# Both row-form attention products of groups 3 to 8 back to back, with three PSUM pairs in rotation

## The chip, the cores and the metric

One core of one Trainium2 chip. The metric is the device time of one execution in microseconds (us), lower is better. "Span" is the time from the first to the last instruction in a trace; it is about 1.8 us less than the timed value of the same execution. All runs told here were in the fast state, at a mean granted clock (the share of its full clock that TensorE was given) of 0.988 or more, and every kernel that ran gave the correct result.

## The reference

An attention without softmax, then a two-layer network with ELU. Batch 8, 8 heads, 576 positions, head size 64; 4608 tokens of 512 features, hidden size 2048.

```python
kv  = np.einsum('bhsd,bhse->bhde', k, v)
out = np.einsum('bhsd,bhde->bhse', q, kv)
rms = np.sqrt(np.mean(out * out, axis=-1, keepdims=True) + 1e-06)
x   = (out / rms * g_norm)              # per head; then tokens x 512
h   = x @ w_in                          # 512 -> 2048
g   = np.where(h > 0, h, np.exp(np.minimum(h, 0)) - 1)
y   = g @ w_out                         # 2048 -> 512
```

## The kernel before

The tokens are worked in nine groups T = 0 to 8 of 512. A "window" of group T holds its first matrix product (eight pairs of feature tiles M0 to M7, `mm1`; a pair is 2 x 128 of the 2048 hidden features, eight matmuls of 512 columns), the second product of group T-1 and half of its own (`mm2_half`, eight matmuls each), and the attention of group T+1: the kv product of batch T+1, and two attention products, halves h = 0 and 1 of the group ("row form": tokens in the PSUM partitions). Each half is squared (ScalarE, ACT), summed (VectorE, DVE), turned into an inverse root (ACT) and scaled (DVE); the scaled rows are transposed by DMA and multiplied by the gain (DVE). A group's tokens can lie in two batches, because a batch has 9 slots of 64 positions and a group 8 slots. Where a pair of slots lies in two batches, its matmul of shape 64x128 (rows x columns of the array in use) is made as two of shape 64x64:

```python
def se_mm(T, h, se_ps):
    for i in range(2):
        (b0, j0), (b1, j1) = (slot_of(T, 4 * h + 2 * i + t) for t in range(2))
        parts = [(0, P, b0, j0, 2)] if b0 == b1 else [(0, 64, b0, j0, 1), (64, P, b1, j1, 1)]
        for m in range(4):
            u, s = m // 2, m % 2
            for l in range(2):
                for lo, hi, b, j, n in parts:
                    nc.tensor.matmul(
                        se_ps[lo:hi, l, (4 * i + m) * 64 : (4 * i + m) * 64 + 64],
                        lhsT=qT[b][l * 64 : l * 64 + 64, s, u, j : j + n, :],
                        rhs=kv_of(b, l, u, s), start=True, stop=True)
```

In PSUM, where matmuls leave their results, the kernel holds tiles of 512 columns: pairs A and B for feature tiles, one pair (here called C, tag "at") for all attention products, two single tiles for the second product's output. The window, shortened:

```python
def window(T, at, early, late, second, relu=(), opened=()):
    for i in range(8):
        ...                                       # (group 2 has its first pair half done)
        rest = mm1(T, i, "BA"[i % 2], i in relu)  # matmuls, then ACT's exp (and relu)
        for name in early.get(i, ()): at[name]()
        if i in second: second[i]()
        rest()                                    # DVE's part of the ELU
        for name in late.get(i, ()): at[name]()

# groups 3 to 7; group 2 has its own lists
early = {2: ("sum0", "inv0"), 4: ("sum1", "inv1"), 5: ("gain0",), 7: ("gain1",)}
late  = {0: ("kv",), 1: ("se0",), 2: ("mul0",), 3: ("se1",), 4: ("mul1", "ahead")}
halves = {0: 1, 1: 3, 2: 4, 3: 5, 4: 6, 5: 7}
# "ahead": DMA transposes of q of batch T+2, then a load of batch T+3
```

## Time and profile before

| | before |
|---|---|
| time, median of the 4 runs beside the changed kernel | 285.95 us (285.7 to 286.31) |
| span of the profiled run | 284.3 us |
| TensorE busy | 97% |
| chain that ended last on TensorE | 84% |

The lines behind the last two are in the prediction. The profile by window follows: length in us, then the busy time of each engine with its instruction count, granted clock, share of the DMA engines, GB/s. The stretches are the windows of groups 2 to 7, from the first matmul of M0 to the next.

```profile
70.72:96.20 25.48, 24.55 (x223) 12.20 (x225) 16.65 (x23) 15.17 (x21) 5.69 (x10) 1.00 0.98 187
96.20:125.53 29.33, 29.03 (x230) 13.52 (x233) 19.78 (x23) 13.57 (x19) 6.64 (x13) 1.00 0.88 175
125.53:154.99 29.46, 29.20 (x236) 13.63 (x240) 18.34 (x22) 13.58 (x19) 5.39 (x11) 1.00 0.72 153
154.99:184.32 29.33, 29.17 (x229) 13.54 (x232) 18.88 (x23) 13.57 (x19) 4.06 (x8) 1.00 0.67 158
184.32:213.78 29.46, 29.20 (x236) 13.63 (x240) 18.59 (x22) 13.58 (x19) 0.00 (x0) 1.00 0.28 66
213.78:242.30 28.52, 28.36 (x157) 12.92 (x160) 18.59 (x22) 13.21 (x18) 0.00 (x0) 1.00 0.28 56
```

The first busy column is TensorE. Groups 3 and 5 take 29.33 us, groups 4 and 6 0.13 us more: their attention has eight matmuls more, for slots in two batches. Group 7 has no kv product. Some matmul records are missing from some traces, which is why counts of equal windows differ by a few; the lengths don't depend on it.

### The profile page before, as it was taken

What the parts mean: (1) busy time and instruction counts of PE and PEld (TensorE: products, weight loads), DVE (VectorE), ACT (ScalarE), POOL (GpSimd) and SP (SyncE); (2) the same over time, 40 slices, a digit from 0 to 9 for tenths busy, and PEclk for the clock granted to TensorE, in tenths of its full rate; (3) what the DMA queues carried; (4) which work ended last, traced back from release to release, by engine and by line L of the source; (5) the groups of instructions that cost most, each with busy time, mean ns of one, the idle gap of its engine ahead of it and who ended that gap; (6) DMA issues with size and microseconds to landing.
All of it is one profiled execution on the core that took longest, in us unless ns stands there. A gap on an engine that the chain in (4) does not pass through costs nothing.

```text
span 284.3 us, 5120 instructions
## 1 busy us (share of the span) xinstructions
PE 274.6 (97%) x2089; PEld 129.1 (45%) x2123; DVE 164.8 (58%) x222; ACT 141.5 (50%) x209; POOL 49.9 (18%) x89
## 2 busy tenths in 40 slices
PE   7899999999899999999999999999999999999994
PEld 3434444444544444444444444444444444444443
DVE  3449532877567657754785378627863786344600
ACT  3778359594568255435542555345543554333311
POOL 7743303341034033032103210000000000000000
PEclk9999999999999999999999999999999999999999
DMA  7999999997999889679637971712150234020222
GB/s 209 193 204 206 205 260 240 202 246 113 184 273 145 165 204 226 83 173 264 149 37 173 256 165 34 157 37 74 39 111 0 74 39 111 0 76 0 74 74 75
DMA packets 50571, 39.46 MB, mean 139 GB/s; under 512 B 30964, under 2 KB 44020, under 8 KB 50548
## 3 DMA queue, kind: packets, MB, share of 16 engines
q0 software_dynamic: 15008, 21.30, 37.4%
q1 hardware_dynamic: 35136, 17.31, 29.5%
q10 hardware_dynamic: 404, 0.53, 0.5%
q8 instruction: 16, 0.26, 0.4%
q14 instruction: 7, 0.06, 0.1%
HBM read 36.70 MB, written 9.44 MB: 162 GB/s over the span
## 4 chain that ended last, share of the span: by engine, by line
PE 84%; DMA 7%; DVE 3%; SPq 2%; issue 1%; ACT 1%; POOL 0%; DVEq 0%; POOLq 0%
PE h_ps L382 39%; PE o_ps L403 39%; DMA w_in_sb<-in_moe_w_in_dram 3%; DMA v_bf<-in_v_dram 2%; DMA qT<-q_bf 2%; PE at L250 2%; PE at L156 1%; PE o_ps L440 1%; PE h_ps L569 1%; DVE xs L299 1%; DVE ss L283 1%; SPq L331 1%; DVE gT L366 1%; DVE elu_e L362 1%; PE qt_ps L174 0%
## 5 line engine op out<-in xcount | busy, mean ns | idle before, releaser
L403 PE MATMUL o_ps<-w_out_sb,gT 128*128 128x512 bf16 x548 | 128.5, 379 | 0.7 <-issue 0.2
L382 PE MATMUL h_ps<-xT,w_in_sb 128*128 128x512 bf16 (+1 forms) x540 | 126.4, 376 | 1.0
L350 ACT ACTIVATE elu_e<-h_ps 128x1024 bf16<-128x1024 f32 (+1 forms) x79 | 74.0, 952 | 89.6 <-PE h_ps L382 78.4
L403 PEld LDWEIGHTS <-gT 128*128 128x128 bf16 x560 | 54.3, 98 | 66.0 <-issue 0.9
L366 DVE TENSOR_TENSOR gT<-elu_e,h_ps 128x1024 bf16<-128x1024 bf16 (+1 forms) x67 | 77.2, 1157 | 6.9 <-PE h_ps L382 0.5
L382 PEld LDWEIGHTS <-w_in_sb 128*128 128x128 bf16 x560 | 53.2, 98 | 61.1 <-issue 0.2
L362 DVE TENSOR_SCALAR elu_e<-elu_e 128x1024 bf16<-128x1024 bf16 x72 | 31.4, 437 | 65.1 <-ACT elu_e L350 65.0
L419 ACT COPY o_sb<-o_ps 128x512 f32<-128x512 f32 x32 | 18.3, 587 | 20.8 <-PE o_ps L403 20.1
L103 POOL CAST q_bf<-st_q 128x384 bf16<-128x384 f32 x36 | 18.5, 557 | 37.6 <-DMA st_q<-in_q_dram 37.6
L283 DVE TENSOR_REDUCE ss<-sq 128x16 f32<-128x1024 bf16 x14 | 17.1, 1218 | 7.7 <-ACT sq L277 7.7
L299 DVE TENSOR_TENSOR xs<-at,ss 128x1024 bf16<-128x1024 f32 x14 | 17.1, 1219 | 1.9 <-ACT ss L292 1.9
L277 ACT ACTIVATE sq<-at 128x1024 bf16<-128x1024 f32 x14 | 14.4, 1029 | 1.1 <-PE at L250 1.1
L212 DVE SCALAR_TENSOR_TENSOR xT<-y_ps,g_col,rT 128x512 bf16<-128x512 f32 (+1 forms) x10 | 6.2, 641 | 10.2 <-ACT rT L209 7.9
L339 POOL COPY gate<-qT 1x16 bf16<-1x16 bf16 x5 | 1.1, 218 | 60.4 <-DMA qT<-q_bf 60.4
L355 ACT ACTIVATE elu_h<-h_ps 128x1024 bf16<-128x1024 f32 (+1 forms) x12 | 9.3, 817 | 0.0
L156 PEld LDWEIGHTS <-k_bf 64*64 64x64 bf16 x576 | 6.4, 107 | 5.4 <-issue 5.4
L90 POOL DMA_DIRECT2D v_bf<-in_v_dram x11 | 7.8, 708 | 4.2 <-DMA w_in_sb<-in_moe_w_in_dram 2.1
L90 POOL DMA_DIRECT2D k_bf<-in_k_dram x11 | 7.9, 718 | 3.1 <-DMA w_in_sb<-in_moe_w_in_dram 2.4
L312 DVE TENSOR_SCALAR xT<-xT,g_col 128x1024 bf16<-128x1024 bf16 x14 | 6.7, 480 | 1.9 <-DMA xT<-xs 1.9
L250 PEld LDWEIGHTS <-qT 64*128 64x128 bf16 (+1 forms) x248 | 4.5, 97 | 7.1 <-issue 5.9
L250 PE MATMUL at<-kv_sb,qT 64*128 64x64 bf16 (+1 forms) x248 | 6.5, 193 | 0.8 <-DMA qT<-q_bf 0.7
L366 DVE TENSOR_TENSOR gT<-elu_e,elu_h 128x1024 bf16<-128x1024 bf16 x9 | 6.5, 723 | 0.8
(57 smaller groups left out, 94.8 us busy)
## 6 DMA issues: line engine op xcount, KB each, us to landing
st_q<-in_q_dram POOLq DMA_DIRECT2D x6, 1152.0 KB, 8.1
out_dram<-o_sb SPq DMA_DIRECT2D x24, 256.0 KB, 3.4
k_bf<-in_k_dram POOLq DMA_DIRECT2D x6, 576.0 KB, 10.6
v_bf<-in_v_dram POOLq DMA_DIRECT2D x6, 576.0 KB, 13.3
out_dram<-o_sb SPq DMA_DIRECT2D x19, 128.0 KB, 2.4
w_out_sb<-in_moe_w_out_dram POOLq DMA_DIRECT2D x4, 512.0 KB, 15.0
w_in_sb<-in_moe_w_in_dram POOLq DMA_DIRECT2D x2, 512.0 KB, 11.2
q_bf<-in_q_dram POOLq DMA_DIRECT2D x3, 288.0 KB, 13.4
```

The lines of the kernel that those rows point to most:

```text
L90: eng.dma_start(out=dst.rearrange("p m j d -> p m (j d)"), in_=in_[:, ms, :])
L103: nc.gpsimd.tensor_copy(out=bf["q", b][:, u, js], in_=raw[b][:, u::2, js, :].rearrange("p l j d -> p j l d"),)
L250: nc.tensor.matmul(se_ps[lo:hi, l, (4 * i + m) * 64 : (4 * i + m) * 64 + 64], lhsT=qT[b][l * 64 : l * 64 + 64, s, u, j : j + n, :], rhs=kv ...
L277: nc.scalar.activation(sq, st["se", h], AF.Square)
L283: nc.vector.reduce_sum(out=ss, in_=st.pop(("sq", h)).rearrange("p l (m e) -> p (l m) e", e=D), axis=AX.X,)
L299: nc.vector.tensor_tensor(out=st["xs"][:, 2 * h : 2 * h + 2, :].rearrange("p i (l m e) -> p l i m e", l=2, e=D), in0=se_ps.rearrange("p l ...
L350: nc.scalar.activation(e[:, lo:hi, :], h, AF.Exp)
L362: nc.vector.tensor_scalar(out=e, in0=e, scalar1=1.0, scalar2=1.0, op0=ALU.min, op1=ALU.subtract)
L366: nc.vector.tensor_tensor(out=gT[T][:, 2 * i + lo : 2 * i + hi, :], in0=e[:, lo:hi, :], in1=h, op=ALU.add if relu else ALU.max,)
L382: nc.tensor.matmul((ps[a] if isinstance(ps, list) else ps[:, a, :])[:, cols], lhsT=w_in_sb[:, c, f * P : f * P + P], rhs=xT[T][:, c, cols] ...
L403: nc.tensor.matmul(o_ps[T, j], lhsT=gT[T][:, f, j * P : j * P + P], rhs=w_out_sb[:, f, :], start=(f == 0), stop=(f == FC - 1),)
L419: nc.scalar.copy(o_sb[T, half][:, j % 2, :], o_ps[T, j])
```

## The change

Intent: make both attention products of a window one block, after three feature pairs (four in group 2), so that TensorE changes between the wide 128-row matmuls and the 64-row attention matmuls once per window instead of twice. The two halves then need two PSUM pairs at once; one is C, the other is A (B in group 2), and in return C takes one feature pair, so that A, B and C rotate. The core of the diff, shortened:

```diff
-        def se(h):
-            def product():
-                st["se", h] = at_tile()
+        def se(h):
+            def product(tag="C"):
+                st["se", h] = pair(tag, "se_ps")
                 se_mm(T, h, st["se", h])
+
+            def square():
                 ...
-    def window(T, at, early, late, second, relu=(), opened=()):
-        ...
+    def window(T, steps):
+        for step in steps.split():
+            # M<i><pair>: first product and exp; R: with relu on ACT; E<i>: DVE's part of the ELU
+            # H<n>/h<n>: eight matmuls of the second product, of group T-1 / T
+            # K<batch><pair>: kv product; G<h>: gain; Q: transposes of q, next loads
+            # X<pair>: both products (half 0 in <pair>, half 1 in C), sq0 sq1 sum0 sum1 inv0 inv1
+            # Y: both scales and their DMA transposes
+        if T == 2:
+            steps = "M0B K3C E0 M1A H5 E1 M2B E2 R3A H6 E3 XB Y H7 Q M4A E4 h0 R5B E5 M6C G0 E6 M7A G1 E7 h2"
+        elif T + 1 < NT:
+            steps = f"M0B {kv} H1 E0 M1A H3 E1 M2B H4 E2 H5 XA Y H6 Q M3B H7 E3 M4A E4 M5C E5 M6B G0 E6 M7A G1 E7 h0 h2"
```

(The comments on the steps are added here; in the source the letters are the branches of an if.) The last group's window keeps its order.

More of the change, by code (lines that the diff above doesn't have):

```diff
@@ L124, in load_w_out @@
         )
-    def at_tile():
-        return ps_at.tile([P, 2, 512], FP32, name="at", tag="at")
     def single(tag, name):
@@ L135, in pair @@
             return [single(t, name) for t in (tag + tag)[:2]]
+        if tag == "C":
+            return ps_at.tile([P, 2, 512], FP32, name=name, tag="at")
         return ps_m1.tile([P, 2, 512], FP32, name=name, tag=tag)
@@ L256, in se_mm, with kv_all @@
                         )
+    def kv_all(b, tag):
+        kv_ps = pair(tag, "kv_ps")
+        for u in range(2):
+            kv_mm(b, [kv_ps[:, s, :] for s in range(2)], u)
+        return lambda: nc.scalar.copy(
+            kv_sb[:, b], kv_ps[:, :, 0:P].rearrange("p s (u e) -> p u s e", u=2)
+        )
     def attention(T):
         st = {}
-        def kv():
-            if T == B:
-                return
-            kv_ps = at_tile()
-            for u in range(2):
-                kv_mm(T, [kv_ps[:, s, :] for s in range(2)], u)
-            nc.scalar.copy(
-                kv_sb[:, T], kv_ps[:, :, 0:P].rearrange("p s (u e) -> p u s e", u=2)
-            )
         def se(h):
-            def product():
-                st["se", h] = at_tile()
+            def product(tag="C"):
+                st["se", h] = pair(tag, "se_ps")
                 se_mm(T, h, st["se", h])
+            def square():
                 sq = attp.tile([P, 2, DM], BF16, name="sq", tag="sq")
@@ L318, in gain @@
                 )
-            return product, sums, inv, scale, gain
-        pieces = {"kv": kv}
+            return product, square, sums, inv, scale, gain
+        pieces = {}
         for h in range(2):
-            for name, piece in zip(("se", "sum", "inv", "mul", "gain"), se(h)):
+            for name, piece in zip(("se", "sq", "sum", "inv", "mul", "gain"), se(h)):
                 pieces[f"{name}{h}"] = piece
@@ L710 @@
         if i == 3:
-            at["kv"]()
+            kv_all(2, "C")()
         if i == 4:
             at["se0"]()
+            at["sq0"]()
             freed[4]()
@@ L725 @@
     at["se1"]()
+    at["sq1"]()
     freed[7], rest[7] = elu(1, 7, ps, "later")
@@ L750 @@
     at["gain1"]()
-    def window(T, at, early, late, second, relu=(), opened=()):
-        for i in range(8):
-            if i < len(opened):
-                mm1_part(T, i, opened[i], range(KC), slice(256, 512))
-                rest = elu(T, i, opened[i], False)
-            else:
-                rest = mm1(T, i, "BA"[i % 2], i in relu)
-            for name in early.get(i, ()):
-                at[name]()
-            if i in second:
-                second[i]()
-            rest()
-            for name in late.get(i, ()):
-                at[name]()
@@ L769 @@
-    for T in range(2, NT):
-        at, early, late = {}, {}, {}
-        if T + 1 < NT:
-            at = attention(T + 1)
-            if T + 2 < B:
-                cast_q(T + 2)
-                def ahead(b=T + 2):
-                    turn_q(b)
-                    if b + 1 < B:
-                        after_turn(b)
-                        fetch_ahead(b + 1)
-                at["ahead"] = ahead
-            else:
-                at["ahead"] = lambda: None
-            early = {2: ("sum0", "inv0"), 4: ("sum1", "inv1"), 5: ("gain0",), 7: ("gain1",)}
-            late = {0: ("kv",), 1: ("se0",), 2: ("mul0",), 3: ("se1",), 4: ("mul1", "ahead")}
-        if T == 2:
-            early = {2: ("sum0", "inv0"), 5: ("sum1", "inv1", "mul1"), 6: ("gain0",), 7: ("gain1",)}
-            late = {0: ("kv",), 1: ("se0",), 2: ("mul0",), 4: ("se1",), 5: ("ahead",)}
-        halves = {1: 5, 3: 6, 5: 7} if T == 2 else {0: 1, 1: 3, 2: 4, 3: 5, 4: 6, 5: 7}
-        second = {i: (lambda n=n: mm2_half(T - 1, n)) for i, n in halves.items()}
-        if T > 2:
-            window(T, at, early, late, second)
-        else:
-            g_tile(T)
-            opened = [pair("B", "h_ps")]
-            mm1_part(T, 0, opened[0], range(KC), slice(0, 256))
-            window(T, at, early, late, second, (3, 5), opened)
-        mm2_half(T, 0)
-        mm2_half(T, 2)
@@ new lines, in mm1_rest @@
+    def mm1_rest(T, i, tag, relu):
+        mm1_part(T, i, opened, range(KC), slice(256, 512))
+        return elu(T, i, opened, relu)
+    def window(T, steps):
+        rest = {}
+        nxt = attention(T + 1) if T + 1 < NT else None
+        for step in steps.split():
+            kind, arg = step[0], step[1:]
+            if kind in "MR":
+                i, tag = int(arg[0]), arg[1]
+                make = mm1_rest if T == 2 and i == 0 else mm1
+                rest[i] = make(T, i, tag, kind == "R")
+            elif kind == "E":
+                rest.pop(int(arg))()
+            elif kind == "H":
+                mm2_half(T - 1, int(arg))
+            elif kind == "h":
+                mm2_half(T, int(arg))
+            elif kind == "K":
+                kv_all(int(arg[0]), arg[1])()
+            elif kind == "X":
+                nxt["se0"](arg)
+                nxt["se1"]("C")
+                for name in ("sq0", "sq1", "sum0", "sum1", "inv0", "inv1"):
+                    nxt[name]()
+            elif step == "Y":
+                nxt["mul0"]()
+                nxt["mul1"]()
+            elif step == "Q":
+                b = T + 2
+                if b < B:
+                    turn_q(b)
+                if b + 1 < B:
+                    after_turn(b)
+                    fetch_ahead(b + 1)
+            elif kind == "G":
+                nxt[f"gain{arg}"]()
+            else:
+                raise ValueError(step)
@@ new lines @@
+    g_tile(2)
+    opened = pair("B", "h_ps")
+    mm1_part(2, 0, opened, range(KC), slice(0, 256))
+    for T in range(2, NT):
+        if T + 2 < B:
+            cast_q(T + 2)
+        if T == 2:
+            steps = "M0B K3C E0 M1A H5 E1 M2B E2 R3A H6 E3 XB Y H7 Q M4A E4 h0 R5B E5 M6C G0 E6 M7A G1 E7 h2"
+        elif T + 1 < NT:
+            kv = f"K{T + 1}C" if T + 1 < B else ""
+            steps = (
+                f"M0B {kv} H1 E0 M1A H3 E1 M2B H4 E2 H5 XA Y H6 Q M3B H7 E3 M4A E4 M5C E5 M6B G0 E6 M7A G1 E7 h0 h2"
+            )
+        else:
+            steps = "M0B H1 E0 M1A H3 E1 M2B H4 E2 M3A H5 E3 M4B H6 E4 M5A H7 E5 M6B E6 M7A E7 h0 h2"
+        window(T, steps)
```

## The prediction

> **What bounds the kernel now.** I read the page first: busy shares, the slices, the chain that ended last.
>
> ```profile
> PE 274.6 (97%) x2089; PEld 129.1 (45%) x2123; DVE 164.8 (58%) x222; ACT 141.5 (50%) x209; POOL 49.9 (18%) x89
> PEclk9999999999999999999999999999999999999999
> PE 84%; DMA 7%; DVE 3%; SPq 2%; issue 1%; ACT 1%; POOL 0%; DVEq 0%; POOLq 0%
> ```
>
> TensorE (PE) is busy in 97% of the 284.3 us span, at a granted clock that never falls, and carries 84% of the final chain. DVE and ACT have 40 to 50% of their time free. So a change can only gain what TensorE does not spend on streaming columns. Next I read the waits of TensorE. After the start-up, one is left:
>
> ```profile
> PE at L250 <- DMA qT<-q_bf: 0.7, 1, 0.7
> ```
>
> Then the TensorE timeline, one group's window at a time. A window of group T holds eight pairs of feature tiles (call them M0 to M7, 8 matmuls each, L382), the second matrix product of group T-1 and the start of T's own (pieces of 8, L403), the kv product of batch T+1 (L156) and the two attention products of group T+1 (L250, halves h=0 and h=1).
>
> ```profile
> 75.01 1.89 PE L403 MATMUL o_ps<-w_out_sb,gT 128*128 128x512 bf16 x8
> 76.83 0.75 PE L250 MATMUL at<-kv_sb,qT 64*128 64x64 bf16 x13
> 78.26 0.28 PE L250 MATMUL at<-kv_sb,qT 64*64 64x64 bf16 x11 [0.68 <-DMA qT<-q_bf]
> 78.47 3.63 PE L382 MATMUL h_ps<-xT,w_in_sb 128*128 128x512 bf16 x15
> ...
> 102.19 1.89 PE L403 MATMUL o_ps<-w_out_sb,gT 128*128 128x512 bf16 x8
> 104.01 0.41 PE L250 MATMUL at<-kv_sb,qT 64*128 64x64 bf16 x16
> 104.35 1.90 PE L382 MATMUL h_ps<-xT,w_in_sb 128*128 128x512 bf16 x8
> 106.09 1.89 PE L403 MATMUL o_ps<-w_out_sb,gT 128*128 128x512 bf16 x8
> ```
>
> Columns: start, length, what. Eight matmuls take 106.09 - 104.35 = 1.74 us where an attention block stands ahead, 1.727 elsewhere (start to start 0.216 us each in the trace). At full load 102.19 + 1.727 = 103.92 would be the next start; the block starts at 104.01. So entering the block leaves 0.096 us (last matmul to first of the block 0.312 instead of 0.216). Leaving it, the last small matmul is followed after 0.123 us, where inside the block small matmuls follow each other every 0.0145 us: another 0.108. The windows are otherwise full: for group 3 it lasts 125.53 - 96.20 = 29.33 us, of which 128 x 0.2158 = 27.62 are wide matmuls.
>
> The first part, at 76.83, is the one real hole: the block takes 78.47 - 76.83 = 1.64 us where the same block of 24 matmuls elsewhere takes 0.48 (140.69 to 141.17). It waits 1.16 us for the transposed q of batch 3, which lands about 78.2.
>
> **What the Trainium skill says.** "TensorE: Matmul & The Clock Gate", section "Wait — 56ns, not 53.3ns?", gives 215.7 ns between 512-column matmuls at full clock; the trace has 0.216, so there is nothing to gain inside the runs. "TensorEngine Tiling (Array Packing)", "Key Properties": changing the tiling mode drains the TensorE. The attention matmuls use 64 rows, the wide ones 128; the 0.096 and 0.108 us at the edges agree. They also match one exposed weight load (98 ns in the load rows), and I cannot tell the two apart here. "Perfetto Trace Analysis" advises rotating independent matmul groups through different PSUM banks so that the evacuation of one overlaps the next. The kernel before does so with two pairs, A and B, for feature tiles, and keeps a third (C) for attention alone; the change lends C to the feature tiles.
>
> **The change part by part.** The built programs have equal counts on every engine: 72 kv matmuls, 32 or 40 attention matmuls, 128 wide ones in a full window. Only order and PSUM pairs change, in the windows of groups 2 to 7 (products of groups 3 to 8); before 76.8 us and in the last group's window TensorE's order is the same. In the windows of groups 3 to 7 the kv block moves ahead of eight matmuls of the second product: same two edges, no cost.
>
> *Removed, in six windows:* one entry and one exit of an attention block, 0.096 + 0.108 = 0.20 us. Check by sum: two blocks of 16 add 2 x (0.312 + 0.217 + 0.123 - 0.216) = 0.87 us to the stream; one of 32 adds 0.312 + 0.450 + 0.123 - 0.216 = 0.67. All on the path, as TensorE has no slack: 6 x 0.20 = 1.22 us.
>
> *Removed, once:* the 1.16 us wait. In the window of group 2 the block now follows M3 and a piece of the second product: it stands at 76.74 + 3 x 1.727 = 81.92, over 3.5 us after q landed.
>
> *Added:* possible waits for PSUM, since the first product (half 0) now sits in a pair that a feature tile needs soon. I laid the vector work of a steady window along the new order, with durations from the rows: ACT elu 1.02, copy 0.59, square 1.03, the two small ACT steps 0.30 and 0.22; DVE elu 0.43 then 1.22 (about 0.1 between), sum 1.22, scale 1.22, gain 0.48. An elu starts 0.20 us after its tile's last matmul has left room for the next, as where TensorE turns to other work at 131.52 and ACT starts at 131.72. Let 0 be the first attention matmul.
> - ACT: copy of the finished output 0.1 to 0.7, squares 0.6 to 1.6 and 1.5 to 2.55. DVE: sums 1.65 to 2.9 and 2.8 to 4.0. Scales 3.95 to 5.15 (frees pair A) and 5.1 to 6.3 (frees C).
> - TensorE: attention to 0.57, then 8 matmuls each: output 2.30, M3 4.03, output 5.76. M4 wants A at 5.76; A is free at 5.15. Margin 0.6 us.
> - M5 wants C at 7.5; free at 6.3. Margin 1.2. ACT takes elu 3 at 4.5 to 5.5, DVE does its part after the scales, 6.3 to 8.0; M6 wants B at 9.2: margin 1.2.
> - M4 ends at 7.5: elu 7.7 to 8.7, DVE 8.75 to 10.5. M7 wants A at 10.95: margin 0.45. M7 ends 12.7; the gain of half 1 ends about 14.6, elu of M7 at 16.2. The next window starts after two output pieces at 16.1 and needs the gain: margin 1.5.
>
> So no wait in groups 3 to 7. In the window of group 2 it is tighter, because only one output piece stands after M7. In trace time: attention 82.0 to 82.7, M4 84.4, the early piece of group 2's own product 86.2, M5 87.9, M6 89.6, M7 91.35 to 93.1, output to 94.8. DVE: M5's relu form ends 92.5, gain 92.9, elu of M6 94.5, second gain 94.95. Group 3's M0 wants the gained input at 94.8: a wait of about 0.2 us, unless the transposed input lands late. It should land about 93.6 (scale ends 88.4, four transposes at 1.27 us in the queue from 87.2, last landing 2.5 us after issue), only 0.9 us ahead of its use.
>
> *Sum:* -1.22 - 1.16 + 0.2 = -2.2 us. 285.7 - 2.2 = 283.5 us, 0.8% less.
>
> **The rivals.**
> 1. *The scale chain takes the place of the gap.* Two squares, two sums and two scales stand in series before M4 can have pair A, where before the change each half had its own 7.3 us between the blocks. For it: the margin is 0.6 us and every step of ACT and DVE adds to it. Against it: all durations are fixed in the rows (the scale is 1217 to 1225 ns in all 14 cases, GpSimd casts beside it or not). If the chain were 1 us longer, M4 would wait 0.4 us in five windows: 285.5 us.
> 2. *Four feature pairs in a row (M4 to M7) make DVE the bound.* TensorE makes one in 1.73 us; DVE needs 1.75 plus two gains of 0.48. For it: the margin at M7 falls to 0.45 us. Against it: the run has only four, and then TensorE does 16 matmuls (3.45 us) that need none of it. If M7 waited 0.5 us in six windows, 3 us come back: 286.5 us.
> 3. *The q wait is hidden or moves.* It is a wait on the engine that bounds, with no idle between it and the end, so its removal shows in full; but the later gain (0.2 us) or the landing of the transposed input could return up to 1 us: 284.3 us.
> 4. *The edges don't shrink*, as two products go to two PSUM pairs: 1.2 us less gain, 284.7 us.
>
> **Range and chances.** The two gains come from measured holes and the engine has no other slack, so I expect nearly all of them. Full removal without any new wait gives 283.3, and the three runs of before lie within 0.6 us of each other, so 282.8 is the lower end. Above lie the margins of rivals 1 and 2; I put the upper end at 284.9. Faster by 2% would need 280.0 us, that is 5.7 us, which the holes do not hold. Slower by 2% (291.4) would need about a microsecond of new waiting in each of the six windows, against margins that are all positive.
>
> **What would show it right or wrong.** Right: the timeline of TensorE has one run of 32 or 40 attention matmuls per window; the line with the 0.68 us wait for q is gone; group 3's window starts about 95.0 instead of 96.20; windows of groups 3 to 7 are 0.2 us shorter (group 3's 29.13 instead of 29.33); the last group's window is unchanged. Wrong: idle of TensorE ahead of the fifth or eighth feature pair with DVE as releaser (rivals 1, 2), a wait over 0.5 us at the first matmul of group 3 (rival 3), or windows of the old length without waits (rival 4).

## The result, and the profile after

| | before | after |
|---|---|---|
| time, median (lowest to highest) | 285.95 us (285.7 to 286.31), 4 runs | 284.06 us (284.03 to 284.22), 4 runs |
| ratio | | 0.9934, 95% interval 0.9917 to 0.9951 |
| span of the profiled run | 284.3 us | 282.2 us |

A ratio is the mean time of one kernel's fast runs over the mean of the other's fast runs of the same rounds, so it is not quite the ratio of the medians. The gain is 1.9 us in the timed runs and 2.1 us between the two traces. All outputs are right. The lengths of equal windows repeat within 0.01 us in a trace, so the small pieces are compared by trace. But a trace is one execution: what comes before group 2's window took 70.52 to 70.92 us in the traces, and the profiled execution need not be a typical one.

The page after the change, its busy line and its chain:

```profile
PE 273.3 (97%) x2094; PEld 129.2 (46%) x2123; DVE 163.9 (58%) x222; ACT 141.6 (50%) x209; POOL 49.1 (17%) x89
PE 92%; DMA 3%; POOL 1%; issue 1%; ACT 1%; DVE 1%; POOLq 0%; DVEq 0%
```

TensorE is as full as before, in a shorter span. The windows of groups 2 to 7, cut at the same events:

```profile
70.63:95.07 24.44, 24.10 (x223) 12.07 (x225) 16.33 (x22) 15.19 (x21) 5.19 (x10) 1.00 0.98 198
95.07:124.18 29.11, 28.85 (x229) 13.53 (x233) 19.55 (x24) 13.57 (x19) 6.89 (x14) 1.00 0.85 176
124.18:153.54 29.36, 29.10 (x239) 13.71 (x241) 18.50 (x23) 13.57 (x19) 5.57 (x10) 1.00 0.67 158
153.54:182.66 29.12, 28.86 (x231) 13.55 (x233) 18.67 (x23) 13.57 (x19) 3.70 (x7) 1.00 0.68 146
182.66:211.90 29.24, 28.98 (x238) 13.65 (x240) 18.28 (x23) 13.57 (x19) 0.00 (x0) 1.00 0.38 72
211.90:240.21 28.31, 28.15 (x158) 12.94 (x160) 18.30 (x23) 13.30 (x18) 0.00 (x0) 1.00 0.25 56
```

Against before: -1.04, -0.22, -0.10, -0.21, -0.22, -0.21 us, in all -2.00. What follows is 42.01 us long in both traces, and the first window begins 0.09 us sooner. So all of the difference but these 0.09 us is in the six windows that the change touches, half of it in group 2. Group 4 gained half of what its neighbours gained; that is the one thing in this table that the prediction does not explain.

TensorE's timeline after the change, around the block in group 2, and then in group 3:

```profile
80.10 1.89 PE L402 MATMUL o_ps<-w_out_sb,gT 128*128 128x512 bf16 x8
81.92 0.88 PE L249 MATMUL se_ps<-kv_sb,qT 64*128 64x64 bf16 x40
...
93.10 1.89 PE L402 MATMUL o_ps<-w_out_sb,gT 128*128 128x512 bf16 x7
95.07 1.89 PE L381 MATMUL h_ps<-xT,w_in_sb 128*128 128x512 bf16 x8
...
108.06 0.64 PE L249 MATMUL se_ps<-kv_sb,qT 64*128 64x64 bf16 x32
...
113.82 7.07 PE L381 MATMUL h_ps<-xT,w_in_sb 128*128 128x512 bf16 x31
```

One run of 40 or 32 attention matmuls stands where two runs stood, with no wait for q, and four feature pairs follow each other without a gap (113.82 on; one of their 32 records is missing). Before the M0 at 95.07 the gap from the last matmul is 0.456 us where 0.216 is the full pace: a wait of 0.24 us. The second gain of the group's input ends just before, as DVE's timeline has it (94.49 + 0.48 = 94.97):

```profile
94.49 0.48 DVE L311 TENSOR_SCALAR xT<-xT,g_col 128x1024 bf16<-128x1024 bf16 x1
...
111.97 2.34 DVE L298 TENSOR_TENSOR xs<-se_ps,ss 128x1024 bf16<-128x1024 f32 x2
```

The second line is the two scales of group 3's window, the first of which frees pair A: it ends at about 111.97 + 1.22 = 113.19, and M4 takes A at 113.82. The margin is 0.63 us, where the prediction had 0.6.

### The profile page after: what moved, and what is told of

Read it like the earlier page. It is cut to its first block, busy times and chain, and to the rows that moved or that the text cites. A ratio compares the mean times of both kernels' runs of the same rounds, so it can differ in the third digit from the quotient of the medians.

```text
span 282.2 us, 5145 instructions
## 1 busy us (share of the span) xinstructions
PE 273.3 (97%) x2094; PEld 129.2 (46%) x2123; DVE 163.9 (58%) x222; ACT 141.6 (50%) x209; POOL 49.1 (17%) x89
## 4 chain that ended last, share of the span: by engine, by line
PE 92%; DMA 3%; POOL 1%; issue 1%; ACT 1%; DVE 1%; POOLq 0%; DVEq 0%
PE h_ps L381 42%; PE o_ps L402 42%; DMA v_bf<-in_v_dram 3%; PE kv_ps L155 2%; PE se_ps L249 2%; PE h_ps L568 1%; PE o_ps L439 1%; POOL k_bf L90 1%; PE qt_ps L173 0%; PE mean L198 0%; PE y_ps L188 0%; POOL v_bf L90 0%; ACT elu_e L349 0%; DVE xT L211 0%; POOL q_bf L90 0%
## 5 line engine op out<-in xcount | busy, mean ns | idle before, releaser
L402 PE MATMUL o_ps<-w_out_sb,gT 128*128 128x512 bf16 x542 | 127.1, 379 | 1.5 <-issue 1.0
L381 PEld LDWEIGHTS <-w_in_sb 128*128 128x128 bf16 x560 | 54.5, 98 | 64.5 <-issue 0.9
L402 PEld LDWEIGHTS <-gT 128*128 128x128 bf16 x560 | 53.5, 98 | 64.0 <-issue 0.9
L361 DVE TENSOR_SCALAR elu_e<-elu_e 128x1024 bf16<-128x1024 bf16 x72 | 32.0, 445 | 59.1 <-ACT elu_e L349 59.0
L282 DVE TENSOR_REDUCE ss<-sq 128x16 f32<-128x1024 bf16 x14 | 16.5, 1214 | 13.0 <-ACT sq L276 13.0
L298 DVE TENSOR_TENSOR xs<-se_ps,ss 128x1024 bf16<-128x1024 f32 x14 | 16.5, 1216 | 1.2 <-ACT ss L291 1.2
L276 ACT ACTIVATE sq<-se_ps 128x1024 bf16<-128x1024 f32 x14 | 13.7, 1030 | 0.3 <-PE se_ps L249 0.3
L155 PE MATMUL kv_ps<-v_bf,k_bf 64*64 64x64 bf16 x576 | 7.5, 194 | 1.0 <-DVE v_bf L112 0.5
L290 ACT ACTIVATE ss<-ss,eps_col 128x16 f32<-128x16 f32 x14 | 4.3, 307 | 6.7 <-DVE ss L282 6.7
```

The costliest lines, as they stand in the source:

```text
L155: nc.tensor.matmul(kv_ps[s][l * 64 : l * 64 + 64, u * 64 : u * 64 + 64], lhsT=bf["k", b][rows, 2 * l + u, j, :], rhs=bf["v", b][rows, 2 * ...
L276: nc.scalar.activation(sq, st["se", h], AF.Square)
L282: nc.vector.reduce_sum(out=ss, in_=st.pop(("sq", h)).rearrange("p l (m e) -> p (l m) e", e=D), axis=AX.X,)
L298: nc.vector.tensor_tensor(out=st["xs"][:, 2 * h : 2 * h + 2, :].rearrange("p i (l m e) -> p l i m e", l=2, e=D), in0=se_ps.rearrange("p l ...
L361: nc.vector.tensor_scalar(out=e, in0=e, scalar1=1.0, scalar2=1.0, op0=ALU.min, op1=ALU.subtract)
L381: nc.tensor.matmul((ps[a] if isinstance(ps, list) else ps[:, a, :])[:, cols], lhsT=w_in_sb[:, c, f * P : f * P + P], rhs=xT[T][:, c, cols] ...
```

## The experiments

Theory: (1) the wait of 1.16 us for q is gone; (2) every change of the array's shape between neighbouring matmuls costs about 0.1 us, and the change removes some; (3) the PSUM rotation only makes room. Rivals: the gain comes from the rotation itself, or the removed wait is hidden anyway. Twelve kernels ran, in three sets of four; the runs of the kernel before beside them had medians of 285.79, 285.77 and 285.95 us, its single runs lay between 284.98 and 287.08.

### The two places apart

Only group 2 in the new order (the old order in groups 3 to 7 is written in the new steps):

```diff
-steps = f"M0B {kv} H1 E0 M1A H3 E1 M2B H4 E2 H5 XA Y H6 Q M3B H7 E3 M4A E4 M5C E5 M6B G0 E6 M7A G1 E7 h0 h2"
+steps = f"M0B H1 E0 {kv} M1A H3 E1 P0C M2B Usum0 Uinv0 H4 E2 Umul0 M3A H5 E3 P1C M4B Usum1 Uinv1 H6 E4 Umul1 Q M5A G0 H7 E5 M6B E6 M7A G1 E7 h0 h2"
```

(P is one product with its square, U one named step.)

> New order in the window of group 2 alone, old order in the windows of groups 3 to 7. Theory (the wait for q goes, and each removed change of tile shape gives about 0.1 us): the window of group 2 is about 1.0 us shorter than before the change (25.5 to 24.4 us), the others are unchanged; span 283.2 to 283.3 us, ratio to before about 0.9963. Rival (the gain is spread evenly over the six windows by the lent PSUM pair): one sixth of 2.0 us, span about 284.0.

Measured: 285.07 us (284.8 to 285.25), ratio 0.9975 (0.9963 to 0.9987), span 283.5. In the trace the window of group 2 is 24.44 us, the others 29.33, 29.46, 29.33, 29.46 and 28.52, as before the change to the hundredth. The rival that spreads the gain is out. The ratio is less far from 1 than I expected (0.9963).

The other way round:

```diff
-steps = "M0B K3C E0 M1A H5 E1 M2B E2 R3A H6 E3 XB Y H7 Q M4A E4 h0 R5B E5 M6C G0 E6 M7A G1 E7 h2"
+steps = "M0B E0 K3C M1A H5 E1 P0C M2B Usum0 Uinv0 E2 Umul0 R3A H6 E3 M4B E4 P1C R5A Usum1 Uinv1 Umul1 H7 E5 Q M6B G0 E6 M7A G1 E7 h0 h2"
```

> Old order in the window of group 2, new order in the windows of groups 3 to 7. Theory: the wait for q stays (block of 24 lasts about 1.6 us), the other windows are shorter by 0.2, 0.1, 0.2, 0.2 and 0.2 us; span 283.3 to 283.5, ratio about 0.997. Rival (the gain is the removed wait alone): span 284.2, as before the change.

Measured: 284.9 us (283.95 to 285.25), ratio 0.9963 (0.9949 to 0.9978), span 283.1. The windows of groups 3 to 7 are 29.16, 29.36, 29.12, 29.25 and 28.30 us, in all 145.19 instead of 146.10. Group 2 keeps its hole:

```profile
76.63 0.65 PE L249 MATMUL se_ps<-kv_sb,qT 64*128 64x64 bf16 x13
77.99 0.28 PE L249 MATMUL se_ps<-kv_sb,qT 64*64 64x64 bf16 x11 [0.71 <-DMA qT<-q_bf]
```

So the gains of the two places add up in the traces to 0.05 us: -1.04 in the first run and -0.91 in the second, against -2.00 with both. (Group 3 took 29.16 us here and 29.11 with both.)

### Is the hole only the late q?

The kernel before, with one call moved:

```diff
     at["mul1"]()
+    turn_q(3)
     store(0, 0)
     ...
-    turn_q(3)
     after_turn(3)
```

> The kernel before, with one edit: the transposes of q of batch 3 are issued ahead of the first stored output instead of behind it (about 1.3 us earlier in the DMA queue). Theory (the hole of 1.16 us is only the late landing of q): block of 24 in the window of group 2 takes about 0.5 us, span 283.1 to 283.4, ratio about 0.996. Rival (the wait is hidden anyway: the gained input of group 3 or something else then holds the next window's start): the hole shrinks but span stays within 0.3 us of 284.3.

Measured: 285.06 us (284.8 to 285.57), ratio 0.9977 (0.9965 to 0.9989), span 283.0.

```profile
76.72 0.54 PE L250 MATMUL at<-kv_sb,qT 64*128 64x64 bf16 x24
77.19 3.63 PE L382 MATMUL h_ps<-xT,w_in_sb 128*128 128x512 bf16 x16
```

The block takes 0.47 us instead of 1.64, and group 2's window is 94.92 - 70.61 = 24.31 us instead of 25.48: the full 1.17 us. The second transpose of q landed at 75.81 us instead of 78.22: it had stood behind a store in the DMA queue. In the trace the wait was not hidden, and its removal needs none of the rotation. In timed runs the moved call gives 0.7 us (by the interval of the ratio 0.3 to 1.0), which is less than the trace's 1.17. The profiled executions differ by 1.29 us (286.09 and 284.8), the medians by 0.73; what the other executions did differently is in no trace, so how long the wait is in a typical run is not shown.

### Are the steady 0.2 us the edges?

Pairs lent as in the change, but eight wide matmuls between the two products:

```diff
-H4 E2 H5 XA Y H6
+H4 E2 P0A Usum0 H5 P1C Usum1 Uinv0 Uinv1 Y H6
```

and in group 2 `XB Y H7` becomes `P0B Usum0 Uinv0 H7 P1C Umul0 Usum1 Uinv1 Umul1`.

> As the changed kernel, both PSUM pairs lent in the same way, but eight wide matmuls stand between the two attention products in every window. Theory (edges): the windows of groups 2 to 7 grow by 0.1, 0.2, 0.1, 0.2, 0.2, 0.2 us against the changed kernel, in all 1.0 us: span 283.2, no TensorE wait for DVE or DMA. Rival (the gain in the steady windows comes from the rotation of three pairs, not from the edges): span 282.2, as the changed kernel.

Measured: 285.79 us (284.95 to 286.58), ratio 1.0003 (0.9987 to 1.002), span 283.5 in the profiled run. In its trace groups 3 to 7 take 146.11 us together, as before the change: the 0.96 us are back. Group 2 takes 24.60 us, with a wait of 0.18 us that the expectation did not have, at M6, whose pair C comes free later here. But the timed runs are up to 1.3 us above the profiled one, at full clock, and I have no trace of one of those. So I ran the split in groups 3 to 7 alone (the edit above, with group 2 left as changed), and the unedited changed kernel beside it as a control.

> The changed kernel once more, unedited, as the control of this set. Expected of all theories: span 282.0 to 282.6, ratio to before about 0.9934; the windows of groups 3 to 7 together 145.1 us.

Control measured: 284.15 us (283.9 to 284.21), ratio 0.9941 (0.9928 to 0.9953), span 282.4, groups 3 to 7 145.15 us.

> As the changed kernel, with eight wide matmuls between the two attention products in the windows of groups 3 to 7 alone; group 2 is left as changed. Theory (edges): those five windows together are 146.1 us instead of 145.1, no TensorE wait, span 283.2, time 0.95 us above the control. Rival (the earlier split was slower in its timed runs for another cause, such as waits that come and go): time more than 1.5 us above the control, or windows with waits in the trace.

Measured: 285.25 us (285.14 to 285.41), ratio 0.9982 (0.9969 to 0.9994), span 283.5; groups 3 to 7 take 29.33, 29.46, 29.33, 29.47 and 28.51 us, in all 146.10, the lengths of the kernel before to 0.01 us, with no wait. Group 3, to be compared with 29.33 before and 29.11 after:

```profile
95.34:124.67 29.33, 28.96 (x230) 13.52 (x234) 19.64 (x24) 13.68 (x19) 7.72 (x14) 1.00 0.85 183
```

That is 1.10 us of time and 0.95 us of trace over the control. In groups 3 to 7, then, three PSUM pairs in rotation with the products apart gain nothing; putting the products together gains all of it. What made the first split kernel slow in some runs stays open. The second one's five runs lie within 0.3 us, which points to group 2's split; but this set ran on another chip than the first, so it is not shown.

### Why group 4 gained only half

In group 4 the slots in two batches are the first of half 1: the joined block is 64x128, then 64x64, then 64x128 again. In the trace the start-to-start gap at these inner changes is 0.120 and 0.125 us; other matmuls of 64x128 come in pairs, 3 ns apart within and 26 ns from pair to pair. Edit: in each block all 64x128 first (shortened; the lines that hand on the two tiles are left out).

```diff
-nxt["se0"](arg)
-nxt["se1"]("C")
+halves = [pair(arg, "se_ps"), pair("C", "se_ps")]
+for n in (2, 1):                  # slots per matmul: 64x128, then 64x64
+    for h in range(2):
+        se_mm(T + 1, h, halves[h], (n,))
```

> The changed kernel, with the attention matmuls of each joined block ordered by tile shape: all of 64x128 first, all of 64x64 last. Theory (every change of tile shape costs 0.1 us, inside a block too): blocks of 40 in the windows of groups 2 and 4 go from 0.81 to 0.71 us, that of group 6 stays; span 0.2 us less than the control. Rival (the gap inside the block belongs to the other q buffer or the other PSUM pair, not to the shape): no change.

Measured: 283.87 us (283.72 to 284.01), ratio 0.9932 (0.9918 to 0.9945), span 282.2. In group 4, TensorE's timeline of the changed kernel:

```profile
137.18 0.88 PE L249 MATMUL se_ps<-kv_sb,qT 64*128 64x64 bf16 x40
137.99 1.25 PE L402 MATMUL o_ps<-w_out_sb,gT 128*128 128x512 bf16 x4
```

and ordered by shape:

```profile
137.27 0.77 PE L249 MATMUL se_ps<-kv_sb,qT 64*128 64x64 bf16 x40
137.97 1.25 PE L403 MATMUL o_ps<-w_out_sb,gT 128*128 128x512 bf16 x4
```

0.81 us becomes 0.70 for the same 40 matmuls. Group 4's window goes from 29.36 to 29.24 us, group 2's from 24.44 to 24.33. A change of shape costs about 0.1 us inside the attention too. Between timed runs the gain is 0.28 us (284.15 to 283.87), at the edge of what can be told.

### The margins: how near were the rivals?

The block one piece later, so that M4 wants pair A 1.73 us sooner after it:

```diff
-H5 XA Y H6 Q M3B H7 E3 M4A
+H5 H6 XA Y Q M3B H7 E3 M4A
```

> The changed kernel with the joined attention block one piece of eight wide matmuls later in the windows of groups 3 to 7, so that the fifth feature pair wants PSUM pair A 1.73 us sooner after it. Theory (the prediction's margin of 0.6 us between the first scale and the fifth pair is real): TensorE waits about 1.1 us for DVE ahead of the fifth pair in each of the five windows, 5.5 us in all, span about 287.8, ratio about 1.013. Rival (the scale is not what frees the pair in time, the margin is far larger): no wait, span 282.4.

Measured: 288.63 us (288.58 to 288.85), ratio 1.0094 (1.0072 to 1.0115), span 286.8.

```profile
110.32 1.90 PE L381 MATMUL h_ps<-xT,w_in_sb 128*128 128x512 bf16 x8
112.06 1.89 PE L402 MATMUL o_ps<-w_out_sb,gT 128*128 128x512 bf16 x8
114.79 2.53 PE L381 MATMUL h_ps<-xT,w_in_sb 128*128 128x512 bf16 x11 [0.84 <-DVE xs L298]
```

112.06 + 1.73 = 113.79 would be M4's start at full pace: it waits 1.00 us for the scale. (The page counts the idle from the modelled end, hence 0.84.) The five waits are 0.76 to 1.00 us, 4.6 in all; I expected 1.1 each. ACT has no output to copy ahead of the squares in this order: the sums start 1.51 us after the block's first matmul (111.26 - 109.75) instead of 1.65 (109.71 - 108.06), so the chain is shorter than I laid it.

M5 in B instead of C, two pairs in rotation after the block:

```diff
-M4A E4 M5C E5 M6B G0 E6 M7A G1 E7
+M4A E4 M5B E5 M6A G0 E6 M7B G1 E7      # A and B swapped in windows 4, 6 and 8
```

> The changed kernel with the sixth feature pair of groups 3 to 7 in B instead of C, so that the last five feature pairs rotate through two PSUM pairs, and the letters A and B swapped in every second window. Theory (the third pair is needed because DVE needs 1.75 us and more for a pair that TensorE makes in 1.73): waits of about 0.5, 0.8 and 0.4 us at the sixth, seventh and eighth pair, 1.8 us a window, 9 us in all; span about 291, ratio about 1.025. Rival (the rotation is not needed): span 282.4.

Measured: 292.78 us (292.66 to 292.84), ratio 1.0237 (1.0211 to 1.0262), span 291.0. Group 3:

```profile
116.08 1.89 PE L381 MATMUL h_ps<-xT,w_in_sb 128*128 128x512 bf16 x8 [0.31 <-DVE gT L365]
118.67 1.89 PE L381 MATMUL h_ps<-xT,w_in_sb 128*128 128x512 bf16 x8 [0.70 <-DVE gT L365]
120.87 1.89 PE L381 MATMUL h_ps<-xT,w_in_sb 128*128 128x512 bf16 x8 [0.31 <-DVE gT L365]
```

Start to start the three waits are 0.48, 0.86 and 0.48 us, in all 1.82, as worked out from the rows (1.8); groups 5 and 7 have the same, groups 4 and 6 have 1.58 and 1.69. So the third pair earns nothing by itself, but without it the joined block costs 8.7 us more.

### Versions that go further

Every change of shape costs, so the kv product (64x64 throughout) should stand directly behind the attention block that ends in 64x64. First try, with k and v fetched a group earlier so that batches 5, 6 and 7 could move:

```diff
+kv_out_ = kv_all(T + 2, "B") if 2 < T < B - 2 else None     # behind both products
 nxt["sq0"](); nxt["sq1"]()
+if kv_out_: kv_out_()
-kv = f"K{T + 1}C" if T + 1 < B else ""
+kv = "K4C" if T == 3 else ""
     load(raw[b], "q", b)
-    for name in "kv":
-        fetch(name, b)
+    for n in {3: (3,), 2: (2,), 4: (4, 5)}.get(b, (b + 1,)):
+        for name in "kv":
+            if n < B: fetch(name, n)
```

> As the run ordered by tile shape, and the kv product of batches 5, 6 and 7 stands directly behind the attention block of the window before, in pair B, with k and v fetched one group earlier. Theory (edges): four shape changes less than in that run, so 0.4 us less than it and 0.6 us less than the control; span about 281.6. Rival (the copy of the kv product holds pair B or k and v land late): a TensorE wait at the fourth feature pair or at the kv product, and a span over the control's.

Measured: 291.46 us (290.17 to 291.81), ratio 1.019 (1.0167 to 1.0213), span 290.0. A miss, by neither of the waits that the rival named:

```profile
93.08 1.89 PE L405 MATMUL o_ps<-w_out_sb,gT 128*128 128x512 bf16 x7
100.66 0.59 PE L384 MATMUL h_ps<-xT,w_in_sb 128*128 128x512 bf16 x1 [5.68 <-DVE xT L314]
```

Group 3's first matmul waits for its gained input; DVE in turn was idle 5.5 us for the DMA transposes of it. Two loads of 576 KB had been put ahead of them, where the DMA engines were 98% busy without them (the share in group 2's window after the change); that these delayed the rows is inferred, and fits the next run, which moves no load and has no such wait. Near the end of the gap the granted clock fell to 0.5, for 6.8 us (99.78 to 106.61). From group 4 on the saving is there: groups 4 to 7 take 114.81 us, 1.11 less than ordered by shape, of which 0.81 is a kv product moved out of this stretch into group 3.

Second try: only batches 6 and 7, whose k and v are there in time without moving a load (otherwise as the run ordered by shape):

```diff
+kv_out_ = kv_all(T + 2, "B") if 3 < T < B - 2 else None     # behind both products
 nxt["sq0"](); nxt["sq1"]()
+if kv_out_: kv_out_()
-kv = f"K{T + 1}C" if T + 1 < B else ""
+kv = f"K{T + 1}C" if T < 5 else ""
```

> As the run ordered by tile shape, with the kv product of batches 6 and 7 alone behind the attention block of the window before, in pair B, and no load moved: k and v of these batches land 1.4 to 1.6 us before their use in the trace of the changed kernel. Theory (edges): three shape changes less than in the run ordered by shape, 0.3 us less than it and 0.5 us less than the changed kernel; span about 281.9, time about 283.6. Rival (k and v are late, or the copy holds pair B): a TensorE wait at the kv product or at the fourth pair of groups 4 and 5, span 282.2 or more.

Measured: 283.52 us (283.42 to 283.64), ratio 0.9914 (0.9895 to 0.9933), span 281.9, as expected, and no wait in groups 3 to 7. In group 4:

```profile
137.22 0.77 PE L249 MATMUL se_ps<-kv_sb,qT 64*128 64x64 bf16 x40
137.82 0.79 PE L155 MATMUL kv_ps<-v_bf,k_bf 64*64 64x64 bf16 x72
```

Here the block ends in 64x64 and the kv product, 64x64 as well, follows after 0.023 us: no cost. In group 5 the block is 64x128 to its end, and the same kv product follows after 0.120 us. Same engine, same two lines of code, operands of the same kind: what differs is the shape of the matmul before. Groups 4 to 6 take 87.31 us, against 87.61 ordered by shape: 0.30 for three changes less. This is the fastest version, 2.4 us under the kernel before and 0.5 to 0.6 under the changed kernel, which ran in the other sets (284.06 and 284.15).

Last, the 0.24 us wait at group 3's start: the first gain of group 2's window put ahead of DVE's part of M5, on top of that version.

```diff
-R5B E5 M6C G0 E6 M7A
+R5B G0 E5 M6C E6 M7A
```

> As the run with kv joined for batches 6 and 7, and the first gain of the window of group 2 stands ahead of the sixth pair's DVE work instead of behind it. Theory (the wait of 0.24 us at the first matmul of group 3 comes from DVE's queue): that wait goes, span 0.2 us less, about 281.7. Rival (the transposed input lands too late for it): the wait stays or grows, span unchanged.

Measured: 284.0 us (283.86 to 284.55), ratio 0.9934 (0.9916 to 0.9952), span 282.2. The rival was right: the wait grew from 0.24 to 0.77 us, and the timed runs are 0.48 us slower.

```profile
91.67 0.48 DVE L312 TENSOR_SCALAR xT<-xT,g_col 128x1024 bf16<-128x1024 bf16 x1 [1.64 <-DMA xT<-xs]
...
94.86 0.48 DVE L312 TENSOR_SCALAR xT<-xT,g_col 128x1024 bf16<-128x1024 bf16 x1
```

DVE now stands idle until the transposed rows are there at 91.67, and everything behind in its queue comes later, the second gain too: 24.27 us after the start of group 2's window (94.86 - 70.59) instead of 23.75 (94.53 - 70.78). It is the second gain that group 3 waits for. Its rows had landed 0.7 us before it began in the version this one started from (93.81 and 94.53), so moving that gain instead is a step that stays untried.

## Why the prediction was right

- **The bound.** Right in the traces: TensorE is the path, and each removed hole showed in full (the q wait 1.17 of 1.16 us when removed alone). In timed runs that one gave 0.7 us, and why is open.
- **"Removed, once: the 1.16 us wait."** Right in size and place, by the traces.
- **"Removed, in six windows: one entry and one exit, 0.20 us", 1.22 in all.** Right in kind, too large by 0.14: the windows lost 1.08. The 0.20 holds in groups 3, 5, 6 and 7 (0.22, 0.21, 0.22, 0.21). In groups 2 and 4 the joined block has a 64x64 part in its middle, so it loses two outer changes of shape and gains an inner one. In changes of shape per window, groups 2 to 7: before 5, 4, 5, 4, 5, 4; after 4, 2, 4, 2, 3, 2. That is ten removed, at 0.1 us 1.0 us, near to what the windows lost besides the q wait and the new wait: 2.00 - 1.16 + 0.24 = 1.08. The inner gaps were already in the trace of the kernel before (0.120 and 0.125 us inside its blocks of 24); I took the block's length as a whole and did not look inside it.
- **"Added: a wait of about 0.2 us" at group 3's start.** Right: 0.24 us, from the work ahead of the second gain in DVE's queue. The rows were not late: the last transpose landed at 93.43 (93.6 predicted), the gain began at 94.49.
- **The margins.** Right, all five: 0.63 us at M4 for 0.6, 1.24 at M5 for 1.2, 1.30 at M6 for 1.2, 0.44 at M7 for 0.45, 1.43 at the next window for 1.5 (group 3, from the rows of TensorE and DVE). Moving the block by 1.73 us turned it into waits of 0.76 to 1.00, and taking the third pair away gave 1.58 to 1.82 us a window for 1.8 worked out. Rivals 1 and 2 of the prediction were near, and it was the third pair and the block's place that kept them off.
- **The total.** 283.5 us predicted, 284.06 measured. Of the 0.56 us, 0.25 is the kernel before itself, whose median in these runs was 285.95 and not the 285.7 that I started from. That part is chance. The rest is the gain: 2.2 predicted, 1.89 in the medians. The traces account for 0.18 of it, 0.14 of overcounted shape changes and 0.04 of the new wait; the other 0.1 is not resolved, as the interval of the ratio allows gains from 1.4 to 2.4 us. The profiled run of before, at 286.09, was 0.14 over that median, which may hold part of it. One sum of the range is loose: with the gain counted, slower by 2% needs (291.4 - 283.5) / 6 = 1.3 us of new waiting in each window, not about one.
- **Left open.** What slowed some runs of the first split kernel; why the timed runs show less than the traces for the q wait alone; and what takes the 0.1 us at a change of shape. The prediction could not tell the array running empty from an exposed weight load, and no run varies one without the other. The records of weight loads narrow it: between the two wide products a load starts 0.214 us ahead of its matmul, at a change of shape the first load starts 0.001 to 0.005 us ahead. So at a change the load is not made ahead, and the 0.1 us passes before it starts; what holds it back is not shown.

## What to carry to other kernels

Where TensorE is full, read its start-to-start gaps, not its busy share: each change of array shape shows there, inside a block of small matmuls as well, and ordering matmuls by shape removed two of them here (0.11 us a block) with no new wait. Before letting a product have a PSUM pair that others need, lay out the chain that frees it along the engine's new order; here a margin of 0.6 us was measured as predicted, and one misplaced piece of eight matmuls would have turned the gain into a loss. In the traces a single transfer standing behind a store in a queue cost 1.17 us, more than five windows of edges (0.96); a look at the waits of the bounding engine finds it, and one moved call removes it.

## What the Trainium skill lacked or had wrong

- "TensorEngine Tiling (Array Packing)", section "Key Properties", says that a change of tiling mode drains the TensorE, and gives no cost. Here each change cost about 0.1 us: 0.312 us instead of 0.216 from a wide matmul to the first small one, 0.120 to 0.125 instead of 0.026 between 64x128 and 64x64, while 64x64 to 64x64 of another product took 0.023. At a change the first weight load starts only 0.001 to 0.005 us ahead of its matmul, 0.214 us between wide products; the page says nothing of that.
- "TensorE: Matmul & The Clock Gate", section "Back-to-back issue gap", gives about 131 ns per matmul at 512 columns as the sustained rate of a stream of weight loads and matmuls. This kernel's streams of such pairs ran at 0.216 us throughout, which is the page's isolated gap.
- "Perfetto Trace Analysis", sections "Optimizing Tensor Performance" and "Matmul Optimizations", advises rotating matmul groups through different PSUM banks and using all eight, without a way to tell how many one product needs. Here the count decided, for the joined block: where DVE needs at least 1.75 us for a pair that TensorE makes in 1.73, two pairs gave 1.58 to 1.82 us of waits a window and three none.
